# Seven products in place of eight for the second half of the first tokens' gates, with the plan of the weight conversions redrawn

## The chip, the core and the metric

The kernel runs on one core of one Trainium2 chip. TensorE (PE) multiplies, with its weight loads (PEld) beside the products; VectorE (DVE) and ScalarE (ACT) do everything elementwise; SyncE (SP) issues nearly all DMAs, in order. The metric is device time in microseconds (us), the median of several executions; one further execution was profiled.

## The reference, cut

```python
# attention: 4 batches, 12 heads, 448 tokens, head size 64, with 12x12 mixes of the heads
scores = mix(scale * q @ k.T, w_pre); attn = mix(softmax(scores), w_post); x = attn @ v   # 1792 x 768
# first feed-forward part, d_ff 1536
y = (sigmoid(x @ w_gate) * (x @ w_val)) @ w_out            # 1792 x 768
# second feed-forward part, d_ff 2048
h = y @ w_in;  out = (h * sigmoid(1.702 * h)) @ w2_out
```

The five feed-forward weights come as 64-bit numbers, and everything is computed in 32 bit.

## The kernel before

After the attention, class `Ffn` works on the tokens in two halves of 2 x 448: `first(0)`, `first(1)`, then `second(1)`, `second(0)`. All is laid out with features on the 128 partitions and 448 tokens in a row.

**Products.** Each 32-bit operand is split into a high part and a rest, and each product is three passes on PE (high by high, high by rest, rest by high). A *block* here is one weight tile `w`, 128 rows x 3 x 128 columns, high and rest. `product` (L871) is the plain form: it uses a block for 18 matmuls of 448 columns. `quarters` (L918) is a form of Strassen's kind: a 2 x 2 arrangement of blocks is done in seven products of sums instead of eight, each block used for 9 matmuls. Its operands are sums of weight blocks (`sum`) and sums of activations (the lists `A[p]`), and its outputs are put together from partial sums in PSUM: ACT copies some out (`save`, L923), DVE adds (`finish`, L927).

**Who uses which form.** In `first(0)` all 12 gate blocks f are plain: 48 weight blocks, tiles `pg` and `pv`. `first(1)` uses `quarters` for its six pairs of f, 84 blocks. `py` (w_out) is plain for both halves, 24 blocks each. `second` uses `quarters` for w_in (four groups of 14 blocks each time) and another form of seven products, `po`, for w2_out.

**Where a block comes from.** A weight piece is loaded as 64-bit words into `ws` (`stage`, five buffers), converted to 32 bit (ACT twice in `bits`; DVE three times in `conv1` to `conv3`), stored to DRAM as `kept`, and, if it is used at once, split by ACT (`high`) and DVE (`low`, L807) into `w` (five buffers). 136 pieces are converted in all. Pieces that are not used at once (`whole(.., False)`) are only stored, between those that are; for `first(0)` these are pieces of w2. Later uses load `kept` again. An order written out in `__init__` (`units`) fixes all of this, and `split`, called by `ahead` after each product, emits it some blocks ahead of PE. Each engine runs its list in order.

`sums_out` makes sums of w2_out's blocks in `first(1)` and `second(1)` and stores them; `next_a` and `next_y` make the lists `A` for the next stage.

## Time and profile before

| what | value |
|---|---|
| median of 3 runs | 1388.9 us (1388.85 to 1389.53) |
| the profiled execution, its own time | 1390.18 us |
| its span, first to last instruction | 1388.1 us |
| PE busy, of the span | 1367.1 us, 98% |
| DVE busy | 1049.7 us, 76% |
| ACT busy | 891.1 us, 64% |
| 16 DMA queues of q1, share of the span | 54.5% |
| bytes moved | 242.36 MB |
| TensorE clock granted | 0.999 |

The profiled execution is 1.3 us longer than the median. An engine's busy time counts an instruction from its start to the end of its writes, and the starts of neighbours overlap the ends, so the distance between two starts is what an instruction costs in a dense row.

### The profile page before, as it was taken

How to read it: one execution, taken by the hardware profiler on the slowest of the kernel's cores; microseconds unless marked ns; L12 is line 12 of the kernel's file. 1: busy time of each engine (PE TensorE's matmuls, PEld its weight loads, DVE VectorE, ACT ScalarE, POOL GpSimd, SP SyncE). 2: the span in 40 equal slices, each digit the busy share in tenths (PEclk: the TensorE clock that was granted, in tenths of full speed). 3: DMA queues.
4: the chain of work that ended last, by engine and by line, in shares of the span. 5: the costliest groups of instructions: out<-in, count | busy, mean ns of one | idle time of the engine just before them, and what ended most of it. 6: DMA issues, size and time to landing. Idle time of an engine off the chain costs nothing.

```text
span 1388.1 us, 26019 instructions
## 1 busy us (share of the span) xinstructions
PE 1367.1 (98%) x8976; PEld 1248.3 (90%) x8976; DVE 1049.7 (76%) x2425; ACT 891.1 (64%) x2087; POOL 168.2 (12%) x159
## 2 busy tenths in 40 slices
PE   7999999999999999999999999999999999999998
PEld 5888888888888999999999988999889999999998
DVE  5777677867888788887868888785877679567654
ACT  5877688878888677676755555563666355566352
POOL 2443344434430000000000000000000000000000
PEclk9999999999999999999999999999999999999999
DMA  6644534622536588887973542683652587222574
GB/s 155 193 139 131 153 126 132 198 98 73 167 116 209 176 292 270 277 294 253 301 245 101 175 140 70 212 281 114 197 167 69 164 268 255 65 69 74 158 252 154
DMA packets 213699, 242.36 MB, mean 175 GB/s; under 512 B 69420, under 2 KB 201280, under 8 KB 213568
## 3 DMA queue, kind: packets, MB, share of 16 engines
q1 hardware_dynamic: 212544, 240.47, 54.5%
q8 instruction: 70, 1.15, 0.3%
q14 instruction: 61, 0.50, 0.1%
q10 hardware_dynamic: 960, 0.23, 0.1%
q0 software_dynamic: 64, 0.01, 0.0%
HBM read 149.04 MB, written 53.08 MB: 146 GB/s over the span
## 4 chain that ended last, share of the span: by engine, by line
PE 84%; DVE 8%; ACT 3%; DMA 2%; issue 2%; POOL 0%; SPq 0%; DVEq 0%; ACTq 0%; POOLq 0%
PE pq L918 20%; PE po L1312 15%; PE py L871 13%; PE pso L328 8%; PE pg L871 6%; PE pv L871 6%; PE psp L283 5%; PE psv L347 5%; PE psq L243 5%; ACT ex L297 1%; DMA gt<-sc 1%; PE pst L208 1%; DVE st L290 1%; DVE w L807 1%; DMA xy<-kept 1%
## 5 line engine op out<-in xcount | busy, mean ns | idle before, releaser
L918 PE MATMUL pq<-xy,w 128*128 128x448 f32 x1764 | 361.8, 366 | 3.4 <-DVE w L807 3.4
L918 PEld LDWEIGHTS pq<-xy,w 128*128 128x128 f32 x1764 | 330.3, 188 | 34.4 <-DVE w L807 6.2
L1312 PE MATMUL po<-wf,xy 128*128 128x384 f32 x1200 | 209.3, 336 | 0.0
L1312 PEld LDWEIGHTS po<-wf,xy 128*128 128x128 f32 x1200 | 209.0, 188 | 0.1
L276 POOL TENSOR_TENSOR ghl<-gt,ghl 120x448 fp32r<-120x448 f32 (+1 forms) x143 | 163.5, 1148 | 240.6 <-ACT ghl L212 179.3
L328 PEld LDWEIGHTS pso<-w,ex 120*112 120x112 f32 (+1 forms) x1440 | 159.3, 177 | 23.2 <-ACT w L310 6.5
L871 PE MATMUL py<-xy,w 128*128 128x448 f32 x864 | 175.1, 364 | 0.0
L328 PE MATMUL pso<-w,ex 120*112 120x120 f32 (+1 forms) x1440 | 172.6, 270 | 2.5 <-ACT w L310 1.6
L871 PEld LDWEIGHTS py<-xy,w 128*128 128x128 f32 x864 | 162.0, 187 | 12.8
L283 PE MATMUL psp<-ghl,wphl 120*120 120x448 f32 x540 | 140.2, 385 | 1.4 <-DVE at L212 0.8
L290 DVE TENSOR_REDUCE st<-psp 120x1 f32<-120x448 f32 x180 | 109.0, 614 | 33.6 <-PE psp L283 32.9
L297 ACT ACTIVATE ex<-psp,st 120x448 f32<-120x448 f32 x180 | 113.2, 635 | 10.7 <-DVE st L290 3.6
L745 ACT ACTIVATE wc<-ws 128x384 f32<-128x384 f32 x136 | 75.5, 555 | 67.0 <-DMA ws<-in_moe_w_in_dram 26.2
L899 ACT CAST xy<-xy 128x384 fp32r<-128x384 f32 (+1 forms) x176 | 79.3, 472 | 42.9 <-DVE xy L1044 42.8
L283 PEld LDWEIGHTS psp<-ghl,wphl 120*120 120x120 f32 x540 | 89.3, 183 | 14.2 <-issue 2.0
L900 DVE TENSOR_TENSOR xy<-xy 128x384 fp32r<-128x384 f32 (+1 forms) x176 | 85.6, 504 | 14.3 <-ACT xy L899 13.9
L871 PE MATMUL pg<-xy,w 128*128 128x448 f32 x432 | 90.3, 366 | 0.0
L871 PE MATMUL pv<-xy,w 128*128 128x448 f32 x432 | 89.5, 365 | 0.0
L871 PEld LDWEIGHTS pv<-xy,w 128*128 128x128 f32 x432 | 81.2, 188 | 6.4
L871 PEld LDWEIGHTS pg<-xy,w 128*128 128x128 f32 x432 | 80.9, 188 | 6.5
L212 ACT CAST ghl<-gt 120x448 fp32r<-120x448 f32 (+1 forms) x131 | 73.7, 569 | 13.1 <-PE psp L283 9.8
L347 PEld LDWEIGHTS psv<-at,vt 112*64 112x64 f32 x1536 | 73.7, 137 | 5.4 <-issue 2.5
(91 smaller groups left out, 1940.2 us busy)
## 6 DMA issues: line engine op xcount, KB each, us to landing
gt<-sc SPq DMA_DIRECT2D x172, 210.0 KB
kept<-wc SPq DMA_DIRECT2D x136, 192.0 KB
ws<-kept SPq DMA_DIRECT2D x68, 384.0 KB
wf<-sb SPq DMA_DIRECT2D x64, 384.0 KB
ws<-in_moe_w_out_dram SPq DMA_DIRECT2D x56, 384.0 KB
ws<-in_moe_w_in_dram SPq DMA_DIRECT2D x32, 384.0 KB
sb<-xy SPq DMA_DIRECT2D x32, 384.0 KB
wf<-kept SPq DMA_DIRECT2D x64, 192.0 KB
```

The costliest lines, as they stand in the source:

```text
L276: eng.tensor_tensor(out=t[:m, 1], in0=gt.pop(s)[:m], in1=t[:m, 0].bitcast(F32), op=ALU.subtract)
L283: nc.tensor.matmul(ps[:m, :S], wphl[:m, wp, :m], t[:m, gp], start=(i == 0), stop=(i == 2))
L290: nc.vector.tensor_reduce(out=st[:m, 0:1], in_=pre[s][:m, :S], axis=AX.X, op=ALU.max, negate=True)
L297: nc.scalar.activation(t[:m], pre.pop(s)[:m, :S], AF.Exp, bias=st[:m, 0:1], scale=1.0, accum_out=st[:m, 1:2])
L328: nc.tensor.matmul(ps[:JC, c, :, :n], e[:m, c * JC:(c + 1) * JC], w[:m, :, :n], start=True, stop=True)
L347: nc.tensor.matmul(ps[a * 64:a * 64 + 64, r, :n], vt[b][:, g, c, :], a_t[:, c, g, :n], start=(c == 0), stop=(c == NJ - 1), tile_position=( ...
L745: self.nc.scalar.activation(c.bitcast(F32), st[:, :, 1].bitcast(F32), AF.Abs, scale=self.DOWN)
L871: self.nc.tensor.matmul(acc[hb][:, :self.S], st, act[k0 + kc][hb][:, ap], start=(k0 + kc == 0 and part == 0 and ap == 0), stop=(k0 + kc == ...
L899: self.nc.scalar.copy(dst[:, 0], src)
L900: self.after(n, lambda: self.nc.vector.tensor_tensor(out=dst[:, 1], in0=src, in1=dst[:, 0].bitcast(F32), op=ALU.subtract))
L918: nc.tensor.matmul(x, st, A[p][c][:, ap], start=(first and c + part + ap == 0), stop=(c == self.KG - 1 and part == 1), skip_group_check=no ...
L1312: nc.tensor.matmul(acc[:, :PW], x[:, part], w[:, wp], start=(start and part == 0 and wp == 0), stop=(stop and part == 1), skip_group_check ...
```

## The change

1. Only the first six f of `first(0)` stay plain (`DIRECT`). The other six go as three groups of `quarters`, with a list `A` for these tokens (`widen`). Their 24 weight pieces (`early`) are converted during the first six f and the first groups, stored, and loaded back as whole groups into four activation-sized blocks (`lift`); `own_sum` makes the weight sums in place there. The six groups of `first(1)` use the same way.
2. The conversions of w2 move later: three in the last group of `first(0)`, 13 beside its `py`, three in each group of `first(1)`, and 30 beside the second `py`.
3. The gate outputs of f = 0 and 1 (`SPILL`) are stored to DRAM (`gd`), loaded back before `py`, and split there; `py` uses them last.
4. In `quarters` the order of the seven products is 1, 5, 6, 2, 7, 3, 4. Product 1 is copied by ACT into the PSUM bank of output 2, and products 2 and 4 end in PSUM, where ACT or DVE reads them directly: two adds of DVE instead of four for each gate or value (in `second(0)` the first two groups keep an add for product 2).
5. `sums_out` of `first(1)` is spread over 38 places instead of 55 and ends by f = 5.

```diff
-    ORDER = (1, 2, 6, 5, 7, 4, 3)
+    SPILL = 2
+    DIRECT = 6
+    ORDER = (1, 5, 6, 2, 7, 3, 4)
...
+        def kept_own(j, others):
+            loads = [[4 * (j + f) + 2 * g for f in range(2)] for g in range(2)]
+            after = max(where[i + x] for y in loads for i in y for x in range(2)) + 2
+            self.groups.append((loads, after))
+            n = len(self.groups) - 1
+            spread = [len(others) * min(x, 8) // 8 for x in range(15)]
+            for x, (p, g) in enumerate((p, g) for p in self.ORDER for g in range(2)):
+                self.used.append(len(self.units))
+                self.units.append(("o", (n, g), p))
+                convert(*others[spread[x]:spread[x + 1]])
+
+        early = [*range(4 * D, o1)]
+        for i in range(4 * D):
+            where[i] = len(self.units)
             whole(i)
-            if 6 <= i < o1 and (i % 3 or i in (12, 36)) or i > o1 + 4 and i % 2:
-                whole(rest.pop(0), False)
+            if i >= 5 and i % 3:
+                convert(early.pop(0))
+        for n, j in enumerate(range(D, K1, 2)):
+            m = (6, 5, 0)[n]
+            convert_now = [early.pop(0) for _ in range(min(m, len(early)))]
+            if j == K1 - 2:
+                convert_now += [rest.pop(0) for _ in range(3)]
+            kept_own(j, convert_now)
...
+    def lift(self):
+        n = len(self.kblocks)
+        if n < min(self.allowed, len(self.groups)) and self.step > self.groups[n][1] and len(self.blocks) >= 4 + self.spare:
+            self.kblocks.append([[self.form(F32) for _ in range(2)] for _ in range(2)])
+            for mine, loads in zip(self.kblocks[n], self.groups[n][0]):
+                for x, i in zip(mine, loads):
+                    self.nc.sync.dma_start(x[:, :, :self.PW], self.kept[i // 2].rearrange("a p f -> p a f"))
...
+    def keep_gate(self, t, f, h, x):
+        if f < self.SPILL:
+            self.nc.sync.dma_start(self.gd[t][f][h], x)
+        else:
+            self.G[f][h] = self.form()
+            self.spare -= 1
+            self.hilo(self.G[f][h], x)
...
-                if bank == 1:
-                    save(q, p)
-                if p == 2:
+                if p == 1 and seeded:
+                    acc[q][2] = self.banks("pq", 1)[0]
+                    nc.scalar.copy(acc[q][2][:, :S], x)
+                elif p in (1, 5, 6):
+                    save(q, p, x)
+                elif p == 2 and seeded:
+                    done(q, 0, 0, x)
+                elif p == 2:
                     finish(q, 1, x, 0, 0)
                 elif p == 7:
-                    finish(q, 7, acc[q][5][:, :S], 1, 1, x)
-                elif p == 4:
-                    finish(q, 7, x, 0, 1)
+                    finish(q, 5, x, 1, 1)
                 elif p == 3:
                     finish(q, 6, x, 1, 0)
+                else:
+                    done(q, 0, 1, x)
...
+    def widen(self):
...
+        def sums(c):
+            (x1, x3), (x2, x4) = ((x[:, 0], x[:, 1]) for x in raw[c])
+            self.tt(x4, x3, x4, ALU.add)
+            self.tt(x3, x1, x3, ALU.subtract)
+            self.tt(x1, x4, x1, ALU.subtract)
+            self.tt(x2, x2, x1, ALU.subtract)
```

On PE the attention and all later stages keep their rows. The end of `first(0)` and what follows stood so before (`pg`, `pv` are gates and values, the `pq` of L918 are the groups of `first(1)`):

```order
L871 MATMUL pg<-xy,w 128x448 x36
L871 MATMUL pv<-xy,w 128x448 x36
L871 MATMUL py<-xy,w 128x448 x432
L918 MATMUL pq<-xy,w 128x448 x756
L871 MATMUL py<-xy,w 128x448 x432
```

and now, after six pairs of such `pg` and `pv` rows where there were twelve:

```order
L956 MATMUL pg<-xy,w 128x448 x36
L956 MATMUL pv<-xy,w 128x448 x36
L1011 MATMUL pq<-xy,w 128x448 x378
L956 MATMUL py<-xy,w 128x448 x432
L1011 MATMUL pq<-xy,w 128x448 x756
```

Twelve rows of 36 matmuls have become one of 378.

On DVE, in the first six f of `first(0)`, this stood from one gate's product with its value (`sg`) to the next block (`w`); `wc` are the conversions:

```order
L894 TENSOR_TENSOR sg<-sg,pv 128x448 x2
L758 SCALAR_TENSOR_TENSOR wc<-wc,ws 128x384
L753 TENSOR_SCALAR wc<-wc 128x384
L764 SCALAR_TENSOR_TENSOR wc<-ws,wc 128x384
L900 TENSOR_TENSOR xy<-sg,xy 128x448 x2
L758 SCALAR_TENSOR_TENSOR wc<-wc,ws 128x384
L753 TENSOR_SCALAR wc<-wc 128x384
L764 SCALAR_TENSOR_TENSOR wc<-ws,wc 128x384
L807 TENSOR_TENSOR w<-wc,w 128x384
```

and now this (the `xy<-xy` rows are `widen`: four sums, and the rests of its splits):

```order
L993 TENSOR_TENSOR xy<-xy 128x448 x2
L979 TENSOR_TENSOR sg<-sg,pv 128x448 x2
L795 SCALAR_TENSOR_TENSOR wc<-wc,ws 128x384
L790 TENSOR_SCALAR wc<-wc 128x384
L801 SCALAR_TENSOR_TENSOR wc<-ws,wc 128x384
L993 TENSOR_TENSOR xy<-xy 128x448 x2
L993 TENSOR_TENSOR xy<-sg,xy 128x448 x2
L795 SCALAR_TENSOR_TENSOR wc<-wc,ws 128x384
L790 TENSOR_SCALAR wc<-wc 128x384
L801 SCALAR_TENSOR_TENSOR wc<-ws,wc 128x384
L878 TENSOR_TENSOR w<-wc,w 128x384
L1141 TENSOR_TENSOR xy<-xy 128x448 x4
```

The conversions are as dense as before, and `widen`'s rows stand between them.

On SP, in the same stretch, stores of converted pieces and loads of the next ones alternated:

```order
L767 DMA kept_116<-wc 128x384
L735 DMA ws<-in_moe_w_out_dram 128x768
L767 DMA kept_69<-wc 128x384
L735 DMA ws<-in_moe_w_gate_dram 128x3x256
L767 DMA kept_117<-wc 128x384
```

Now the loads of a whole group come between, soon after the store that fills the last of its pieces (and, elsewhere in the stretch, 12 loads `xy<-xd` for `widen`):

```order
L804 DMA kept_76<-wc 128x384
L772 DMA ws<-in_moe_w_gate_dram 128x3x256
L804 DMA kept_69<-wc 128x384
L772 DMA ws<-in_moe_w_gate_dram 128x3x256
L852 DMA xy<-kept_73 128x2x384
L852 DMA xy<-kept_75 128x2x384
L852 DMA xy<-kept_74 128x2x384
L852 DMA xy<-kept_76 128x2x384
L804 DMA kept_77<-wc 128x384
```

The loads of `kept_73` to `kept_76` stand ahead of the next pieces' loads, and the last of them reads what was stored four rows above the first.

## Rows read from the trace of the kernel before

**Rows 1.** The page: span, and busy time of each engine

```profile
span 1388.1 us, 26019 instructions
PE 1367.1 (98%) x8976; PEld 1248.3 (90%) x8976; DVE 1049.7 (76%) x2425; ACT 891.1 (64%) x2087; POOL 168.2 (12%) x159
```

**Rows 2.** The chain that ended last: start, length, engine, tile, line, instructions

```profile
468.12 7.30 PE pv L871 x36
...
635.93 87.40 PE py L871 x432
...
1177.61 102.42 PE pq L918 x504
```

**Rows 3.** Waits of PEld, 723 to 880 us: total, times, longest

```profile
PEld pq L918 <- DVE w L807: 2.5, 4, 1.1
```

**Rows 4.** Timeline of PEld, 723 to 1075 us: idle before a piece in brackets

```profile
805.28 25.59 PEld L918 LDWEIGHTS pq<-xy,w 128*128 128x128 f32 x126 [0.68 <-DVE w L807]
...
833.83 45.43 PEld L918 LDWEIGHTS pq<-xy,w 128*128 128x128 f32 x223 [1.08 <-DVE w L807]
...
989.47 1.71 PEld L918 LDWEIGHTS pq<-xy,w 128*128 128x128 f32 x9 [2.22 <-DVE w L807]
```

**Rows 5.** Waits of PEld, 967 to 1073 us

```profile
PEld pq L918 <- DVE w L807: 3.7, 4, 2.2
```

**Rows 6.** Timeline of DVE, 521.8 to 526.9 us: start, length

```profile
521.38 0.62 DVE L894 TENSOR_TENSOR sg<-sg,pv 128x448 f32<-128x448 f32 x1
521.91 0.55 DVE L758 SCALAR_TENSOR_TENSOR wc<-wc,ws 128x384 uint32<-128x384 uint32 x1
522.38 0.36 DVE L753 TENSOR_SCALAR wc<-wc 128x384 f32<-128x384 f32 x1
522.65 0.55 DVE L764 SCALAR_TENSOR_TENSOR wc<-ws,wc 128x384 uint32<-128x384 uint32 x1
523.12 0.55 DVE L807 TENSOR_TENSOR w<-wc,w 128x384 fp32r<-128x384 f32 x1
523.58 0.56 DVE L758 SCALAR_TENSOR_TENSOR wc<-wc,ws 128x384 uint32<-128x384 uint32 x1
```

**Rows 7.** `low` (L807) on DVE: stretch, length, busy (count), clock, DMA share, GB/s

```profile
0.00:504.60 504.60, 7.75 (x14) 1.00 0.49 153
...
0.00:577.50 577.50, 19.40 (x35) 1.00 0.54 169
```

**Rows 8.** Matmuls of `product` (L871) on PE by the same times

```profile
0.00:504.60 504.60, 44.75 (x217) 1.00 0.49 153
...
0.00:577.50 577.50, 117.65 (x577) 1.00 0.54 169
```

**Rows 9.** Busy time by stretch: PE, PEld, DVE, ACT, POOL; then clock, DMA share, GB/s

```profile
519.00:548.00 29.00, 29.00 (x144) 26.88 (x144) 24.65 (x56) 19.65 (x43) 0.00 (x0) 1.00 0.81 270
...
679.00:708.00 29.00, 29.00 (x146) 26.87 (x145) 24.84 (x55) 19.92 (x44) 0.00 (x0) 1.00 0.96 314
705.00:710.00 5.00, 5.00 (x26) 4.64 (x25) 1.88 (x5) 2.52 (x6) 0.00 (x0) 1.00 1.06 392
...
775.50:801.50 26.00, 25.79 (x127) 23.40 (x126) 24.15 (x49) 15.71 (x34) 0.00 (x0) 1.00 0.56 173
...
937.00:967.04 30.04, 30.04 (x150) 27.85 (x149) 14.31 (x27) 8.93 (x19) 0.00 (x0) 1.00 0.38 131
```

**Rows 10.** The page's DMA issues: count, KB each

```profile
kept<-wc SPq DMA_DIRECT2D x136, 192.0 KB
...
ws<-in_moe_w_gate_dram SPq DMA_DIRECT2D x24, 384.0 KB
...
xy<-xd SPq DMA_DIRECT2D x24, 224.0 KB
```

**Rows 11.** Timeline of DVE, 966 to 1020 us, one wait for a DMA

```profile
986.17 1.15 DVE L1044 TENSOR_TENSOR xy<-xy 128x384 f32<-128x384 f32 x2 [2.88 <-DMA xy<-kept]
```

**Rows 12.** The chain, two loads that stood in it

```profile
979.89 6.19 DMA xy<-kept
1004.43 4.66 DMA xy<-kept
```

More of the change, by code (lines that the diff above doesn't have):

```diff
@@ L563, in __init__ @@
         for m in range(KD):
-            self.pieces += [self.block(w_out, k0, KG, m * 128, 128) for k0 in range(0, K1, KG)]
+            self.pieces += [self.block(w_out, k0 % K1, KG, m * 128, 128) for k0 in range(KG, K1 + KG, KG)]
         for f in range(K2):
@@ L1131, in first @@
     def first(self, t):
[L1133 to L1134 removed]
+        K1, S, D = self.K1, self.S, self.DIRECT
+        G = self.G = [[None, None] for _ in range(K1)]
         if t:
[L1136 to L1141 removed]
+            self.later_work(self.sums_out(range(3), 3), 38)
+        else:
+            self.A = {p: [] for p in self.ORDER}
+            self.later_work(self.widen(), 4 * D - 7)
+            self.spare = 12
+        for f in range(K1):
+            if t or f >= D:
+                if f % 2:
+                    self.spare = 0 if f < self.SPILL else 4
+                    if f < K1 - 1:
+                        self.allowed += 1
+                    self.gates(t, f - 1, f == K1 - 1)
+                if t and f == 5:
                     self.rush()
[L1143 removed]
+            else:
                 if f == 0:
```

195 lines of the change are left out of this document (138 added, 57 removed).

## The prediction

> **What bounds the kernel.** The page comes first: PE is busy for 1367.1 of 1388.1 us and PEld for 1248.3, while DVE has 76% and ACT 64% [rows 1]. Then the chain of waits, where from 468 us on hardly anything but PE stands: 36 matmuls of a gate or a value take 7.30 us, which is 0.2027 us each, the 432 of `py` 87.40, and 504 of `quarters` without a wait 102.42, which is 0.2032 each [rows 2]. A matmul more or less is therefore worth 0.203 us as long as nothing else stops PE. Third, what does stop it: in `first(1)` PEld waited four times for the rests of weight blocks (`low`, L807), 2.5 us in all [rows 3], in pieces of 0.68 and 1.08 us where one group of seven products passes to the next [rows 4]; in the first groups of `second(1)` four times again, 3.7 us [rows 5], of which 2.22 in one piece [rows 4] that followed a 2.88 us wait of DVE for a load of `sums_out` [rows 11]. In all of these stretches DVE is late, not PE slow.
>
> So DVE's list needs a measure. Its rows overlap at their ends, so I take the distance of starts: 0.47 us for each of the two long steps of a conversion, 0.27 for the short one, 0.46 for a `low`, 0.53 for 448 columns [rows 6]; other operations on 384 columns I take as 0.47. One conversion is 1.21 us. With these I count, block by block in the order of DVE's list, what it must do while PE uses a block (18 matmuls, 3.65 us, in plain products; 9, 1.82 us, in `quarters`).
>
> **What the change takes away.** 12 rows of 36 matmuls go, 432 x 0.2027 = 87.6 us; 378 come, 378 x 0.2032 = 76.8 us. That is -10.8 us, and no other stage gains or loses a matmul.
>
> **What it puts on DVE in `first(0)`.** In the first six f the list was comfortable: in the 13 blocks from the 15th on there stood 22 conversions, 13 `low` and 16 operations of 448 columns, 41.1 us, for 47.4 us of PE. Now the same 13 blocks hold 18 conversions, 15 of 384 columns and 36 of 448 (`widen`'s sums and splits and the sums of the first pair's gates), 47.6 us. The last four of them are blocks of 9 matmuls, so PE needs 9 x 3.65 + 4 x 1.82 = 40.1 us. DVE is 7.5 us over. What it has in hand: at 504.6 us 14 `low` had started where PE had used 217 / 18 = 12.1 blocks, at 577.5 us 35 against 577 / 18 = 32.1 [rows 7, 8], so 2 to 3 blocks, 7.3 to 11 us. A DVE that never waited would just pass. It does wait: in the densest stretch of `first(1)` it was busy for 24.15 of 26.0 us, 93%, and PE waited there [rows 9]. At 95%, 47.6 us become 50, 10 over, and 0 to 2.7 us of PE time are lost; to that come the small waits of a full list. The two groups behind hold 44.4 us for 51; their densest four blocks, 9.1 and 7.5 us for 7.3 of PE, are like the group ends of `first(1)` (9.0 for 7.3), which cost 0.7 to 1.1 us each. I take 3 us for the passage and 1 for the two groups: +4. Bounds: 0, if the hand of 3 blocks holds; 10, if it counts for nothing.
>
> **What it puts on the DMA queues.** In the 20 blocks of f = 1 to 5 SP issues 33 pieces of 384 KB and 33 stores of 192 KB as before, and besides 12 loads and 4 stores of 224 KB and one group of four times 384 KB [rows 10]: 24.7 MB in 73.0 us, 338 GB/s. The busiest long stretch moved 314 GB/s at a share of 0.96 [rows 9], so a full share is some 327, and 24.7 MB take 75.5 us, 2.5 over. That comes out of the same 2 to 3 blocks in hand; a late piece makes ACT wait, then DVE. It is in the +4. The Trainium skill (DMA: Bandwidth & Descriptors, Specifications) gives some 358 GB/s from memory for one core; by that the stretch would take 69.0 us, an estimate, and no load would be late. The trace does not hold to it in the short: 5 us went at 392 GB/s [rows 9]. By that limit the rival without new waits, below, gains.
>
> Beside the first `py` DVE's list grows from 66.8 to 73.5 us of 87.6, and the DMAs to 30.2 MB (35 conversions, 28 transfers of 224 KB, two groups), 92.3 us at 327 GB/s against 87.4 [rows 2]. Five over, seven in hand: I take +0.5, bounds 0 and 5.
>
> **What the new order does to `first(1)` and `second(1)`.** Two adds of four go and two conversions a group come; the sums are 130.6 us before and 131.3 now, of 153. But the heap at the end of a group (nine operations of 448 and nine of 384 columns in four blocks, 9.0 us for 7.3) is taken apart: 6.5 us now. In the first three groups `sums_out`, squeezed into fewer places, gives 8.7 us at worst. I take -0.5 us of the 2.5 lost there, bounds -2 and +3. In `second(1)` the first two groups hold 49.9 us instead of 48.8. More to the point, at the end of the second `py` DVE was idle half the time, 14.31 us busy of 30.04 [rows 9], and now has the last conversions of w2 there: the last four blocks of `py` and the first four behind them hold 24.4 us of work instead of 16.3, for 21.9 of PE. What is queued behind are the splits by `next_y` that product 5, now second, needs 4.9 us after `py` ends. +0.5 us, bounds -1 and +4.
>
> **At nothing**: ACT's copy into PSUM (the third bank is read one pair later, 3.65 us, and a copy was there before); the gates by way of DRAM, used after 9 of 12 steps of `py`, 11 us after it begins; the loads of later groups, issued 7 to 14 blocks, 13 to 25 us, before use, where such a load took 4.7 to 6.2 us [rows 12]. Without that cover each would cost PE what the load in rows 11 did, some 2 us.
>
> **Sum.** -10.8 + 4 + 0.5 - 0.5 + 0.5 = -6.3 us. The profiled execution took 1390.2 us, so 1383.9; it stands 1.3 us above the median, so 1382.6 for the median. Less than 0.2%, 2.8 us, can't be told from no change here.
>
> **The rivals.**
>
> *No new wait.* The three blocks in hand carry DVE over the passage, and the flatter group ends free 1.5 us more: 1388.9 - 10.8 - 1.5 = 1376.6. For it: PE never waited between 468 and 723 us. Against: DVE never had more work than PE there. 17%.
>
> *DVE becomes the bound of `first(0)`.* The hand counts for nothing, since SP, which issues in order, waits for DVE's conversions and the group's stores before the next piece's load; 10 us lost there, 1388. For it: both lists and queues are over at the same blocks. Against: behind the passage the load falls to 44.4 of 51 us. 13%, a little under half of it faster by more than 2.8 us.
>
> *Slower: groups are loaded too late.* ACT runs in order; if its `high` for a group's first block waits for `lift`'s loads, the copies out of PSUM behind it wait too, and PE stops at the product that reuses the bank. The places are the second and third group of `first(0)` and the first of `first(1)`, whose loads follow the conversions they read, in a full queue. At the 6.19 us of the longest load in the chain [rows 12], three cost 18.6 us, 1401; at 4 us each 1394.6. It decides from 2.1 us each on (no gain) and makes the kernel slower by 0.2% from 3 us. For it: store, landing and four loads of 384 KB must pass in 13 us. Against: the first two loads are all that the first blocks need. 12%.
>
> **The numbers.** My forecast has 58%, from 1379 to 1386. The low end of the range is that of the first rival, 1376; the high end, 1389, takes in the second and leaves out the third, 12%, and little else. Faster by over 0.2%: 58 + 17 + 6 = 81%. Within: 7 of the second, 2 of the third, 9%. Slower: 10%.
>
> **What would show it.** One row of 378 matmuls in some 77 us, with `first(0)` from 468 us to the start of `py` in about 161 (168 before). Waits of PE or PEld for `low` between the 15th and the 28th block, near 515 to 560 us, 2 to 4 us together, and few later; none for ACT's copies. DMA share near 1 in f = 1 to 5. Waits in `first(1)` near 2 us, and in the first three groups alone. I am wrong if the wait stands elsewhere (at `xy<-kept`, or at the start of `second(1)` by more than 4 us), if there is none, or if matmuls themselves take longer beside fuller queues.

## The result and the profile after

The changed kernel takes 1407.7 us (1402.9 to 1407.8) against 1388.9 (1388.3 to 1389.5): ratio 1.0127, 95% interval 1.0105 to 1.0149. It is slower by 1.3%, where 0.5% faster was forecast. The profiled execution is the shortest of them, 1402.9 us; what makes the other three 4.8 us longer is open, since they left no trace (their mean granted clocks are 0.990, 0.990 and 0.992, this one's 0.993).

The page of the changed kernel: span, engines, and the row of `py`, with what PE waited for at its end.

```profile
span 1400.9 us, 26068 instructions
...
PE 1362.5 (97%) x8922; PEld 1240.3 (89%) x8922; DVE 1067.2 (76%) x2451; ACT 909.5 (65%) x2135; POOL 168.5 (12%) x159
...
L956 PE MATMUL py<-xy,w 128*128 128x448 f32 x864 | 183.3, 373 | 11.8 <-DVE xy L942 5.9
```

PE is busy for 4.6 us less than in [rows 1], not for 10.8. What stands behind that shows in the stages; a cut at the first weight load of each gives these windows (the columns are those of [rows 9]).

```profile
467.20:634.40 167.20, 160.60 (x776) 146.03 (x775) 145.02 (x307) 109.91 (x235) 0.00 (x0) 0.99 0.70 228
634.40:730.30 95.90, 91.43 (x433) 82.66 (x432) 79.34 (x174) 61.27 (x132) 0.00 (x0) 0.96 0.92 306
730.30:884.40 154.10, 154.10 (x757) 141.82 (x757) 135.13 (x276) 100.83 (x215) 0.00 (x0) 1.00 0.52 174
884.40:983.30 98.90, 91.54 (x433) 82.79 (x433) 73.96 (x157) 52.03 (x112) 0.00 (x0) 0.95 0.81 269
983.30:1085.80 102.50, 102.50 (x506) 94.56 (x505) 76.50 (x158) 67.51 (x150) 0.00 (x0) 1.00 0.44 144
```

From top to bottom: the first tokens' gates, the first `py`, the second tokens' gates, the second `py`, the first product with w2. The stages that were to stay as they were moved most (forecast by the prediction's terms):

| Stage, us | before | after | difference | forecast |
|---|---|---|---|---|
| first tokens' gates, from the first `pv` | 167.8 | 167.2 | -0.6 | -6.8 |
| first `py` | 87.4 | 96.0 | +8.6 | +0.5 |
| second tokens' gates | 156.3 | 154.1 | -2.2 | -0.5 |
| second `py` | 87.4 | 98.9 | +11.5 | 0 |
| first w2 product | 106.0 | 102.5 | -3.5 | +0.5 |
| before and behind these | | | -0.9 | 0 |

The sum is +12.8 up to rounding, the difference of the spans, 1400.9 and 1388.1. The medians lie 18.8 us apart; the 6 us more are the place of the two profiled executions among the others, and the table does not account for them. The two `py` lose 20.0 us. PEld's timeline shows where in the first:

```profile
634.37 10.92 PEld L956 LDWEIGHTS py<-xy,w 128*128 128x128 f32 x54
646.68 0.19 PEld L956 LDWEIGHTS py<-xy,w 128*128 128x128 f32 x1 [1.39 <-ACT xy L944]
647.40 0.19 PEld L956 LDWEIGHTS py<-xy,w 128*128 128x128 f32 x1 [0.53 <-ACT xy L944]
649.82 0.19 PEld L956 LDWEIGHTS py<-xy,w 128*128 128x128 f32 x1 [2.23 <-DVE xy L942]
650.35 1.60 PEld L956 LDWEIGHTS py<-xy,w 128*128 128x128 f32 x5 [0.35 <-DVE xy L942]
653.77 0.29 PEld L956 LDWEIGHTS py<-xy,w 128*128 128x128 f32 x1 [1.81 <-DVE xy L942]
654.30 7.69 PEld L956 LDWEIGHTS py<-xy,w 128*128 128x128 f32 x32 [0.25 <-DVE xy L942]
```

54 matmuls run, nine of the twelve steps of k (10.9 us). The tenth needs gate 0, and PE waits six times, 6.6 us, first for its cast (L944, ScalarE), then for its low part (L942, VectorE). ScalarE in turn waited for the load, and SP issued that load late. SP's, then ScalarE's timeline:

```profile
639.92 0.32 SPq L804 DMA_DIRECT2D kept<-wc  x1
...
640.81 2.54 SPq L1301 DMA_DIRECT2D xy<-gd  x4
```

```profile
646.06 0.56 ACT L944 CAST xy<-xy 128x448 fp32r<-128x448 f32 x1 [4.50 <-DMA xy<-gd]
```

The four loads stand at 640.81, 6.4 us after `py` began, behind stores of converted weights that each wait for VectorE. SP's own waits, 634 to 645 us (total, times, longest):

```profile
SPq L804 <- DVE wc L801: 4.8, 4, 1.9
```

The second `py` repeats it, later still, after waits of 1.9 us for a gate made last (L992, L993; experiment 2); PEld, then SP:

```profile
894.67 0.30 PEld L956 LDWEIGHTS py<-xy,w 128*128 128x128 f32 x2 [1.54 <-ACT xy L992]
895.33 1.71 PEld L956 LDWEIGHTS py<-xy,w 128*128 128x128 f32 x9 [0.36 <-DVE xy L993]
900.86 0.29 PEld L956 LDWEIGHTS py<-xy,w 128*128 128x128 f32 x1 [3.82 <-ACT xy L944]
901.44 0.28 PEld L956 LDWEIGHTS py<-xy,w 128*128 128x128 f32 x1 [0.30 <-ACT xy L944]
904.93 0.29 PEld L956 LDWEIGHTS py<-xy,w 128*128 128x128 f32 x1 [3.20 <-DVE xy L942]
```

```profile
894.18 2.59 SPq L1301 DMA_DIRECT2D xy<-gd  x4
```

The waits are 6.6 and 9.5 us, the losses 8.6 and 11.5. The other 2 us each go with matmuls at a lower clock. Windows of 5 us, first `py`:

```profile
640.00:645.00 5.00, 5.00 (x26) 4.62 (x26) 3.74 (x8) 1.01 (x2) 0.00 (x0) 1.00 0.94 297
645.00:650.00 5.00, 1.79 (x7) 0.83 (x5) 2.16 (x5) 3.79 (x9) 0.00 (x0) 1.00 1.05 380
650.00:655.00 5.00, 3.74 (x9) 2.42 (x10) 5.00 (x13) 3.79 (x8) 0.00 (x0) 0.54 0.83 273
655.00:660.00 5.00, 5.00 (x22) 4.53 (x21) 3.59 (x9) 2.96 (x7) 0.00 (x0) 0.78 0.95 306
660.00:665.00 5.00, 5.00 (x26) 4.65 (x25) 4.93 (x11) 3.61 (x9) 0.00 (x0) 1.00 0.82 261
```

While PE stood for 3.2 of 5 us the granted clock was 1.00; in the next 5 us it was 0.54, which is near the lower level of 1.2 GHz, then 0.78, then 1.00, the upper level of 2.4 GHz, again. In the second `py` it was 0.50 and 0.52 from 900 to 910 us, behind the longest waits. In the kernel before nothing stopped PE in either `py`, and the granted clock of both is 1.00.

In the first tokens' gates the waits stand where they were forecast, from 517 to 563 us, but they are 8.9 us and not 2 to 4, and two of the six are for ScalarE's part of a block (L872) and not for `low` (L878):

```profile
517.21 2.73 PEld L956 LDWEIGHTS pv<-xy,w 128*128 128x128 f32 x14 [1.83 <-DVE w L878]
...
529.64 6.38 PEld L956 LDWEIGHTS pv<-xy,w 128*128 128x128 f32 x32 [1.59 <-DVE w L878]
537.21 3.54 PEld L956 LDWEIGHTS pg<-xy,w 128*128 128x128 f32 x18 [1.20 <-ACT w L872]
543.19 0.70 PEld L956 LDWEIGHTS pg<-xy,w 128*128 128x128 f32 x4 [2.45 <-ACT w L872]
544.27 4.29 PEld L956 LDWEIGHTS pg<-xy,w 128*128 128x128 f32 x14 [0.38 <-DVE w L878]
...
563.36 2.72 PEld L1011 LDWEIGHTS pq<-xy,w 128*128 128x128 f32 x14 [1.41 <-DVE w L878]
```

### The profile page after: what moved, and what is told of

It is laid out like the page before. It is cut to its first block, busy times and chain, and to the rows that moved or that the text cites. A ratio compares the mean times of both kernels' runs of the same rounds, so it can differ in the third digit from the quotient of the medians.

```text
span 1400.9 us, 26068 instructions
## 1 busy us (share of the span) xinstructions
PE 1362.5 (97%) x8922; PEld 1240.3 (89%) x8922; DVE 1067.2 (76%) x2451; ACT 909.5 (65%) x2135; POOL 168.5 (12%) x159
## 4 chain that ended last, share of the span: by engine, by line
PE 57%; DMA 1%; DVE 1%; issue 0%; ACT 0%; SPq 0%; DVEq 0%; ACTq 0%
PE pq L1011 30%; PE po L1468 15%; PE py L956 12%; DMA xy<-gd 1%; DMA ws<-in_moe_w_in_dram 0%; DVE wc L801 0%; DVE wc L795 0%; ACT wc L782 0%; DMA ws<-in_moe_w_val_dram 0%; DVE xy L942 0%; DVE wc L790 0%; DVE w L878 0%; SPq L772 0%; SPq L804 0%; ACT xy L944 0%
## 5 line engine op out<-in xcount | busy, mean ns | idle before, releaser
L1011 PE MATMUL pq<-xy,w 128*128 128x448 f32 x2142 | 436.8, 365 | 1.0 <-DVE w L878 1.0
L1011 PEld LDWEIGHTS pq<-xy,w 128*128 128x128 f32 x2142 | 401.7, 188 | 35.5 <-DVE w L878 1.4
L956 PE MATMUL py<-xy,w 128*128 128x448 f32 x864 | 183.3, 373 | 11.8 <-DVE xy L942 5.9
L956 PEld LDWEIGHTS py<-xy,w 128*128 128x128 f32 x864 | 165.5, 192 | 29.4 <-DVE xy L942 8.1
L992 ACT CAST xy<-xy 128x384 fp32r<-128x384 f32 (+2 forms) x188 | 85.5, 479 | 41.0 <-DVE xy L1141 39.5
L993 DVE TENSOR_TENSOR xy<-xy 128x384 fp32r<-128x384 f32 (+2 forms) x188 | 92.6, 512 | 19.0 <-ACT xy L992 18.8
L1141 DVE TENSOR_TENSOR xy<-xy 128x384 f32<-128x384 f32 (+1 forms) x144 | 79.5, 559 | 6.6 <-DMA xy<-kept 4.8
L347 PE MATMUL psv<-at,vt 112*64 112x120 f32 (+1 forms) x1536 | 77.1, 260 | 0.6 <-ACT ex L297 0.4
L878 DVE TENSOR_TENSOR w<-wt,w 128x384 fp32r<-128x384 f32 x100 | 54.8, 553 | 28.8 <-ACT w L872 28.8
L790 DVE TENSOR_SCALAR wc<-wc 128x384 f32<-128x384 f32 x136 | 48.3, 355 | 37.2 <-ACT wc L782 36.8
```

What stands on the lines that cost most here:

```text
L347: nc.tensor.matmul(ps[a * 64:a * 64 + 64, r, :n], vt[b][:, g, c, :], a_t[:, c, g, :n], start=(c == 0), stop=(c == NJ - 1), tile_position=( ...
L956: self.nc.tensor.matmul(acc[hb][:, :self.S], st, act[k0 + kc][hb][:, ap], start=(k0 + kc == 0 and part == 0 and ap == 0), stop=(k0 + kc == ...
L992: self.nc.scalar.copy(dst[:, 0], src)
L993: self.after(n, lambda: self.nc.vector.tensor_tensor(out=dst[:, 1], in0=src, in1=dst[:, 0].bitcast(F32), op=ALU.subtract))
L1011: nc.tensor.matmul(x, st, A[p][c][:, ap], start=(first and c + part + ap == 0), stop=(c == self.KG - 1 and part == 1), skip_group_check=no ...
L1141: self.nc.vector.tensor_tensor(out=dst, in0=x, in1=y, op=op)
```

## The experiments

Stage times below are cut as in the table above, in its order, so a wait for the first weight of a stage counts to the stage ahead of it. Each is from one execution. What stands ahead of the first `pv` has the same rows in every kernel, and yet `pv` begins anywhere from 465.0 to 471.1 us in the profiled executions, a range of the size by which whole times of one kernel differ (2 to 9 us); the stages leave this out. Each compared kernel keeps all of the change but what its edit says, unless it is put on the kernel before. "Ratio" is to the kernel before, executed beside it (its medians were 1389.8 to 1390.6 us there), with its 95% interval; it is not the quotient of the two medians.

**1. The reload issued sooner (`gates_back_sooner`).** The loads move from behind the last group of gates into it:

```diff
+                    if last is not True and p == last:      # p == 5
+                        self.bring()                        # the four loads of gd
...
-        for f in range(self.SPILL):
-            for h in range(2):
-                G[f][h] = self.form()
-                self.nc.sync.dma_start(G[f][h][:, 1].bitcast(F32), self.gd[t][f][h])
```

> The changed kernel, with one thing moved: the four loads that bring the two spilled gates back are issued inside the last group of gates, after its second product, instead of behind that group's last stores of converted weights. Theory A (the reload is late: it is issued 6.2 and 9.6 us after the first py step begins, ScalarE's cast of it stands ahead of the weights' casts, and TensorE's clock falls while it waits): both py stages go back from 96.0 and 99.2 us to 87.5 to 90 each, no wait of TensorE's loads there is over 0.5 us, and the whole is 15 to 20 us below the changed kernel's 1407.7, so 1388 to 1393. Rival B (the py stages are longer since more conversions lie beside them, 35 and 29 in place of 33 and 19, and the reload only happens to be late): both stages stay above 94 us and the whole at 1400 to 1408.

Measured: 1396.2 us, ratio 1.0046 (1.0030 to 1.0062); stages 168.0, 93.4, 154.2, 93.6, 102.7. The two `py` got back 8 of their 20 us and lie between what the two theories gave. In the first `py` the loads are now in time, and yet the low parts are not. ScalarE, VectorE and PEld:

```profile
646.14 1.03 ACT L944 CAST xy<-xy 128x448 fp32r<-128x448 f32 x2
```

```profile
650.15 1.16 DVE L942 TENSOR_TENSOR xy<-xy 128x448 fp32r<-128x448 f32 x2
...
654.11 1.16 DVE L942 TENSOR_TENSOR xy<-xy 128x448 fp32r<-128x448 f32 x2
```

```profile
654.78 0.29 PEld L956 LDWEIGHTS py<-xy,w 128*128 128x128 f32 x1 [2.51 <-DVE xy L942]
```

ScalarE casts at 646.1 without a wait for the load. VectorE, in the order of its list, comes to the low parts at 650.2 and 654.1, where PE wants gates 0 and 1 from 650.4 on: conversions stand ahead of them, and it was busy for 10.4 of the 11.0 us since `py` began.

**2. No reload (`no_reload`).** Loads, casts and low parts are left out; gates 10 and 11 stand in:

```diff
+        used = G[self.KG:] + [G[10], G[11], G[2]]
...
-            for k, _ in enumerate(self.product(py, act)):
+            for k, _ in enumerate(self.product(py, used)):
```

> The changed kernel without the reload: the gates of blocks 0 and 1 are still stored to DRAM but not brought back, not cast, and gates 10 and 11 are used a second time in their place (this leaves those two gates out of the product with w_out). Everything else stands as in the changed kernel, the conversions beside py too. Theory A: both py stages 87.4 to 88.5 us, the whole 17 to 20 us below the changed kernel, 1387.5 to 1391; what it is faster than the kernel with the loads issued sooner is what the reload costs even when it is in time (I expect under 2 us). Rival B: the stages stay above 94 us, the whole above 1400.

Measured: 1388.9 us, ratio 0.9991 (0.9978 to 1.0004); stages 167.0, 87.4, 155.5, 89.5, 102.7. Both `py`:

```profile
632.20:719.60 87.40, 87.40 (x433) 81.03 (x432) 73.93 (x163) 56.65 (x123) 0.00 (x0) 1.00 0.96 318
875.10:964.60 89.50, 88.05 (x434) 80.95 (x434) 70.42 (x151) 49.38 (x108) 0.00 (x0) 1.00 0.88 287
```

All conversions stand beside `py` as in the changed kernel (73.9 us of VectorE's work in the first), and PE is never without work in the first. So theory A holds and rival B falls: the return of two gates' outputs costs 8.5 and 9.4 us. The expectation that a return in time costs under 2 us falls as well: with the loads sooner the kernel is 7.3 us above this one. The 2.1 us left in the second are a wait for the cast of gate 10, made last and now used eighth.

**3. Casts and low parts sooner too (`gates_split_sooner`).**

```diff
+                    if last == "gates" and p == 7:
+                        self.settle()          # cast and low part of the four blocks
...
-                if m == 0 and k in (self.KG - 1, 2 * self.KG - 1):
-                    for h in range(2):
-                        x = G[k // self.KG][h]
-                        self.part(self.nc.scalar, x, 0)
-                        self.after(0, lambda x=x: self.part(self.nc.vector, x, 1))
```

> The changed kernel with the reload issued inside the last group of gates, as in the run with the loads sooner, and with the reloaded gates' four casts on ScalarE and four low parts on VectorE also put inside that group, behind its fifth product, in place of behind the third and the sixth step of py. Theory A2 (with the loads in time, the waits that stay in py, 3.3 and 5.0 us, are for low parts that stand in VectorE's list behind conversions; VectorE has no idle time from 634 to 660 us, and a low part ends at 651 and 655 us where it is wanted at 650 and 652): both py stages go from 93.4 and 93.6 to 87.5 to 89.5 us, the whole to 1388 to 1391. Rival B (VectorE has too much to do there, wherever the low parts stand): the wait moves to the weights' low parts, and the stages stay at 92 us or more, the whole at 1394 to 1398.

Measured: 1395.2 us, ratio 1.0029 (1.0009 to 1.0049); stages 167.9, 89.1, 156.9, 91.9, 103.2. The two `py` gain 6 us more, as expected of the first, not quite of the second; there one wait of 3.22 us for the cast of gate 10 stays. But the stage behind the first `py` is 2.7 us longer, with three waits, 2.9 us in all, at its start, two of them for VectorE, and the whole time is that of rival B, not clearly below experiment 1, whose interval overlaps: what `py` gained is in part lost behind it.

**4. The new order and the two outputs in PSUM alone (`quarters_only`)**, put on the kernel before:

```diff
-    ORDER = (1, 2, 6, 5, 7, 4, 3)
+    ORDER = (1, 5, 6, 2, 7, 3, 4)
...
+                if p == 1 and seeded:
+                    acc[q][2] = self.banks("pq", 1)[0]
+                    nc.scalar.copy(acc[q][2][:, :S], x)
...
-    EASE = {1: 1.1, 2: 0.4, 6: 2.0, 5: 2.0, 7: 0.5, 4: 0.4, 3: 0.6}
+    EASE = {1: 1.0, 5: 1.0, 6: 2.0, 2: 0.8, 7: 0.8, 3: 0.4, 4: 1.0}
```

`EASE` sets how much of the work in waiting (here `sums_out`) is issued behind each product. It comes with the order, and so does an earlier place of two loads of each group; the changed kernel has both.

> The kernel before, with the new order of the seven products and the two outputs that are summed in PSUM, and nothing else of the change: all first tokens' gates direct, no gate by way of DRAM, the conversions where they were. Theory A: the 2.6 and 3.6 us by which the changed kernel's seven-product stages (gates of the second tokens, first w2 product) are shorter come from this edit, so about 1382 to 1384, ratio 0.995 to 0.9965, and both stages show no wait of TensorE over 0.5 us. Rival B: they come from the kept weights' blocks and the fewer conversions that the other edits leave there; then this is 1388 to 1390, ratio 0.999 to 1.001, and the waits of the kernel before (four of 0.5 to 0.8 us in a group) are still there.

Measured: 1388.0 us, ratio 0.9974 (0.9959 to 0.9989); stages 167.8, 87.4, 156.3, 87.4, 102.8. The w2 product has the whole 3.2 us, in one piece without a wait:

```profile
968.90:1071.70 102.80, 102.80 (x506) 94.67 (x506) 76.37 (x158) 67.75 (x150) 0.00 (x0) 1.00 0.44 143
```

The second tokens' gates have nothing of it: four waits, 2.5 us in all, are there as before, but only two of them still for `low` (now L810). The other two are for ScalarE's sigmoid of a gate (L968). PEld, 725 to 882 us:

```profile
PEld pq L921 <- DVE w L810: 1.5, 2, 0.7
PEld pq L921 <- ACT s L968: 1.0, 2, 0.7
```

Half of each theory: nearly all of the 3.5 us comes from this edit, and the 2.2 us of the gates need the others as well.

**5. The first tokens' gates: four cuts, and two of them together (`light_no_x`).** Each leaves the reload as it is, so the stage tells, not the whole.

```diff
 no_x_loads: sums of the quarters from the high parts in SBUF
-                    self.nc.sync.dma_start(x[:, h], self.xd[h][:, cc, :])
 sums_gpsimd: the sums of widen on another engine
+            tt = lambda dst, x, y, op: self.nc.gpsimd.tensor_tensor(out=dst, in0=x, in1=y, op=op)
 half_early: six of thirteen conversions ahead left out
+                if x // 2 not in (13, 15, 17):
+                    convert(x)
 early_light: conv1 and conv2 left out for all thirteen
+        if self.units[i][0] == "f" and not 24 <= self.units[i][2] < 37:
```

`no_x_loads`:

> The changed kernel, where the sums of the tokens' quarters for the seven products are formed from the rounded high parts that are in SBUF, in place of twelve loads of the whole values from DRAM (this leaves the low parts out of these sums). VectorE's and ScalarE's instructions stay as many and as large; 2.75 MB of transfers between about 490 and 545 us are gone. Theory A (the six waits of 8.9 us in sum there, and the half clock behind them, come from full DMA queues: the share is 0.92 to 0.96 with 304 to 325 GB/s from 468 to 540 us): the stage up to py goes from 167.4 to 157 to 161 us, the whole to 1397 to 1401. Rival B (VectorE's list, 0.96 of the stretch, and the sums of 2.6 us that stand ahead of a conversion): the stage stays at 165 us or more and the whole within 3 us of the changed kernel.

`sums_gpsimd`:

> The changed kernel, with the twelve sums of the tokens' quarters (VectorE, 2.60 us for four) on GpSimd, which does nothing else there; the reload is as in the changed kernel. Theory A (VectorE's list sets the waits of the direct products between 511 and 563 us): 7.8 us of VectorE's work are gone, the waits fall from 8.9 us to under 5 and the stage up to py from 167.4 to 160 to 164, the whole to 1400 to 1404. Rival B (what is late there are the weights' loads: ScalarE waits 3.2 us for one at 533 us, and the transfers were not relieved enough by leaving out the tokens' loads): the stage stays at 166 us or more and the whole within 2 us of 1407.7.

`half_early`:

> The changed kernel, six blocks direct, with six of the thirteen pieces that are converted ahead beside the direct products left out (this puts the values of six other pieces of the gate weights in their place in the seven-product groups). The tokens' sums, loads and parts stay. Theory A (the conversions ahead fill VectorE's list): 6 x 1.4 us = 8.4 us of VectorE's work less in 73 us of products; the waits between 511 and 563 us fall from 8.9 us to under 3 and the stage up to py from 167.2 to 158 to 161 us. Rival B (the tokens' sums and parts, or the loads, make them): the waits stay at 6 us or more and the stage at 164 us or more.

`early_light`:

> The changed kernel with two of VectorE's three conversion instructions left out (0.27 and 0.47 us each) for the thirteen pieces that are converted ahead beside the direct products, so that the weights kept of these have wrong values. Their loads, ScalarE's two instructions, the third of VectorE and the stores stay. Theory A (VectorE's list sets the waits): 9.6 us less of VectorE's work, the transfers as they were; the waits between 511 and 563 us fall from 8.9 us to under 4, and the stage up to py from 167.2 to 158 to 162 us. Rival B (the transfers and the staging buffers of the pieces do it, and leaving out six pieces helped since 3.5 MB went with them): the stage stays at 164 us or more.

`light_no_x`:

> The two earlier cuts together, with six blocks direct and the reload as in the changed kernel: the tokens' twelve loads for the sums left out (the low parts with them), and two of VectorE's three conversion instructions left out for the thirteen pieces converted ahead (their kept values are wrong). Alone, the first took the stage up to py from 167.2 to 166.2 us, the second to 165.2. Theory C (two causes in a row: VectorE's list holds the pieces up to 535 us, and the transfers, with the conversion behind them, hold those from 535 us on; with one of them gone the other still makes ScalarE and the loads late): together 157.5 to 161.5 us, far more than the 164.2 that the two sums give. Rival D (the two add up, and something else, ScalarE's waits for the conversions' chain through the staging buffers, keeps the rest): 163 to 165 us, waits of 6 us or more still there.

Measured, stage up to `py` and waits of 0.3 us or more in it: the changed kernel 167.2 and 8.9; `no_x_loads` 166.2 and 8.1; `sums_gpsimd` 167.4 and 7.3 with the first wait at 500 us; `half_early` 158.0 and 0.9; `early_light` 165.2 and 8.3; `light_no_x` 164.9 and 6.6. Whole times: 1403.2, 1402.6, 1392.2, 1406.1 and 1400.9 us, the last three from one execution each, the first two with ratios of 1.0089 (1.0064 to 1.0114) and 1.0095 (1.0080 to 1.0110).

Only `half_early` does what theory A said, and it has the whole gain: 9.8 of 10.8 us, with one wait of 0.88. So the number of conversions ahead sets the waits. The others have the stages of their second theory (B, or D); the whole times of `no_x_loads` and `sums_gpsimd` are 4.5 and 5.1 us below the changed kernel's median, more than B allowed, and beside its profiled execution, 1402.9, the same. What of a conversion does it is told in part by the others. With less work on VectorE the first two waits shrink from 1.83 and 1.59 to 0.49 and 0.62 (`early_light`), and with the tokens' loads gone too they vanish; those up to 535 us are VectorE's list, helped by the full queue. The later ones stay in both. `light_no_x`, SP, ScalarE and PEld:

```profile
519.36 2.14 SPq L852 DMA_DIRECT2D xy<-kept  x4
...
522.38 0.38 SPq L772 DMA_DIRECT2D ws<-in_moe_w_val_dram  x1
```

```profile
529.60 0.55 ACT L782 ACTIVATE wc<-ws 128x384 f32<-128x384 f32 x1 [3.85 <-DMA ws<-in_moe_w_val_dram]
```

```profile
533.85 3.54 PEld L956 LDWEIGHTS pg<-xy,w 128*128 128x128 f32 x18 [1.32 <-ACT w L872]
539.59 0.71 PEld L956 LDWEIGHTS pg<-xy,w 128*128 128x128 f32 x4 [2.19 <-ACT w L872]
```

SP issues the first group's four loads of 384 KB at 519.4; ScalarE then waits 3.85 us for a piece of w_val, until 529.6, and PE stands until 533.85, and again until 539.59. The changed kernel has ScalarE's wait with 3.21 us, `half_early` with 3.89. There PE does not wait: when ScalarE's wait began, VectorE had finished 1.8 blocks more than PE had used (`low` rows against weight loads / 18), where the changed kernel had 0.7.

The second of these waits of PE has one more cause, the sums that the rival of `no_x_loads` names. VectorE, then ScalarE, in `light_no_x`:

```profile
535.38 2.35 DVE L1141 TENSOR_TENSOR xy<-xy 128x448 f32<-128x448 f32 x4
...
538.38 0.55 DVE L801 SCALAR_TENSOR_TENSOR wc<-ws,wc 128x384 uint32<-128x384 uint32 x1
```

```profile
539.03 0.51 ACT L872 CAST w<-wc 128x384 fp32r<-128x384 f32 x1 [2.59 <-DVE wc L801]
```

VectorE, held up by the late piece, has four sums of the tokens in its list ahead of the next conversion, and ScalarE's cast, for which PE stands until 539.59, waits for that conversion. The same rows of the changed kernel are 2.60 and 2.84 us. In `sums_gpsimd`, where these sums are not on VectorE, PE has no wait of 0.3 us from 531.7 to 558 us.

So theory C falls, and the numbers are those of D, 6 us or more of waits. Its cause is not shown alone: what is left goes with `half_early`, which leaves out six pieces whole (their loads, ScalarE's steps, VectorE's third step, the stores), and which of these does it was not separated. That the four loads alone make ScalarE's wait was not tried either, and stays open.

`sums_gpsimd` did not shorten the stage, since VectorE had no less to do. GpSimd, then VectorE:

```profile
499.84 5.60 POOL L1196 TENSOR_TENSOR xy<-xy 128x448 f32<-128x448 f32 x4 [1.56 <-DMA xy<-xd]
```

```profile
500.29 1.30 DVE L790 TENSOR_SCALAR wc<-wc 128x384 f32<-128x384 f32 x1
501.51 1.52 DVE L801 SCALAR_TENSOR_TENSOR wc<-ws,wc 128x384 uint32<-128x384 uint32 x1
...
505.58 0.55 DVE L801 SCALAR_TENSOR_TENSOR wc<-ws,wc 128x384 uint32<-128x384 uint32 x1
```

While GpSimd works, from 499.8 to 505.4, VectorE's conversion steps of 0.35 and 0.55 us take 1.30 and 1.50. (GpSimd's three groups of four sums took 5.3, 5.6 and 12.1 us.) VectorE is busy for 143.0 us from 468 to 630 where the changed kernel has 140.2.

**6. Eight or ten blocks direct, and the gates' return mended.** The groups of seven products cost a head start of conversions; fewer groups, fewer conversions.

```diff
-    DIRECT = 6
+    DIRECT = 8                                   # or 10
-            if i >= 5 and i % 3:
+            if i >= 5 and i % 2:                 # with 10: i % 4 == 0
 d8_last: gates made last are used last
-        act = G[self.KG:] + G[:self.KG]
+        act = G[3:9] + G[:3] + G[9:]
 d8_last_b: loads behind product 1, casts and low parts behind 2 (fourth), not 5 and 7
```

> The changed kernel with eight blocks of the first tokens' gates direct and four as two groups of seven products, in place of six and three groups: 396 products of a bank in place of 378, so 3.65 us more of TensorE's work, but only 16 pieces to convert ahead in place of 24, and 32 pieces' time for them. The reload is as in the changed kernel. Theory A (the conversions ahead overfill VectorE's list in the direct stretch): its waits fall from 8.9 us to under 3, the stage up to py from 167.4 to 163 to 166 us, the whole to 1402 to 1406. Rival B (the waits come with the sums and parts of the tokens, whenever these are made): the waits stay at 7 us or more and the stage goes to 169 to 171 us, the whole to 1409 to 1412.

> The two together: eight blocks direct, and the reload with its casts and low parts inside the last group of gates. If the two causes are apart from each other the gains add: py 87.5 to 89.5 us each, the stage up to py 163 to 166, the whole 1383 to 1388, ratio 0.996 to 0.999 to the kernel before. If one is only hidden by the other, it stays above 1390.

> Eight blocks direct, the reload with casts and low parts inside the last group of gates, and in py the pieces of w_out in the order gates 3 to 8, 0 to 2, 9 to 11, in place of 3 to 11, 0 to 2, so that the gates that are made last are used last. Theory A3 (what stays in the second py, 91.8 us with one wait of 2.84 us for ScalarE's cast of gate 10, is that the change put the last-made gates at the eighth of twelve steps): the second py goes to 87.5 to 89 us, the whole from 1388.5 to 1384.5 to 1386.5. Rival B (ScalarE's list is late there by itself): a wait of the same size at another tile, and the whole at 1387 to 1390.

> The same with the reload issued behind the first product of the last group, and its casts and low parts behind the fourth, in place of the second and the fifth. If the 1.28 us that TensorE waits at the start of the first py (for a low part of a weight, behind the four low parts of gates) comes from those four standing late in the group, it goes, and the whole is 1 to 2 us below the kernel with the later place; if VectorE's list is full there wherever they stand, the wait moves into the last group and the time is the same within 1 us.

> Ten blocks direct, and one group of seven products for the first tokens: 414 products of a bank, only 8 pieces converted ahead; else as the kernel with eight. Theory A (with eight blocks two waits of some 1.5 us in the first tokens' gates are left to gain, and each group less costs 3.65 us): the stage up to py is 164 to 165 us against 162.4 with eight, the whole 1.5 to 3 us above the kernel with eight. Rival B (the conversions beside the direct products still cost more than the waits show, in py behind them too): the whole is the same or lower.

| Kernel | us | ratio, interval | stages |
|---|---|---|---|
| `direct_8` | 1399.6 | 1.0068, 1.0053 to 1.0084 | 163.0, 95.2, 153.5, 96.9, 103.3 |
| `split_and_direct_8` | 1388.5 | 0.9995, 0.9984 to 1.0006 | 162.4, 88.7, 157.8, 91.8, 103.7 |
| `d8_last` | 1389.2 | 0.9995, 0.9983 to 1.0008 | 163.6, 88.8, 157.2, 90.1, 106.5 |
| `d8_last_b` | 1386.1 | 0.9974, 0.9961 to 0.9986 | 163.5, 87.6, 155.0, 88.7, 105.0 |
| `d10_last` | 1388.0 | 0.9979, 0.9964 to 0.9994 | 164.2, 88.7, 155.1, 89.2, 104.6 |

`direct_8` has the stage and the waits of theory A (3.65 us more of products, 4.2 us less of stage, 2.3 us of waits); its whole time is below the 1402 to 1406 expected. The two causes nearly add: `split_and_direct_8` lies 19 us below the changed kernel, where the gains one by one are 12.5 and 8.1, and just above the range expected. With the order of w_out's pieces (`d8_last`) the wait for gate 10 is gone, and the second `py` itself takes what A3 expected. The 90.1 of the table holds a wait for the first weight of the product behind it. PEld:

```profile
879.75 87.51 PEld L956 LDWEIGHTS py<-xy,w 128*128 128x128 f32 x432
...
969.84 0.34 PEld L1011 LDWEIGHTS pq<-xy,w 128*128 128x128 f32 x2 [2.58 <-ACT w L872]
```

That is rival B, a wait of the same size (2.84 before) at another tile, and the whole is B's too; the stage behind is 2.8 us longer. The earlier place of casts and low parts (`d8_last_b`) has a median 3.1 us lower, with intervals that just touch: this wait is 1.16 there and the stage behind 105.0. The 1.28 us at the start of the first `py` went into the last group of gates, as 0.99, which is the second reading of its expectation; the time is not. `d10_last`, which has the loads and casts where `d8_last` has them, is 1.2 us below that with overlapping intervals, so rival B holds: no gain from eight over ten is shown. Four blocks by seven products save 7.3 us of products; `d8_last_b` is 1.9 us shorter in these five stages than `quarters_only`, and their ratios are equal.

**7. The tokens' parts in the new order.** The change reordered the products and left the order in which the quarters' parts are made.

```diff
 next_y, beside the second py (quarter_a, beside the first, likewise)
-            self.hilo(A[2][c], x)
             self.tt(t1, t1, y, ALU.add)
+            self.hilo(A[5][c], t1)
             self.tt(t0, t1, t0, ALU.subtract)
-            self.flush()
             self.hilo(A[6][c], t0)
+            self.hilo(A[2][c], x)
```

> Eight blocks direct, gates back behind the first and split behind the fourth product, last-made gates last; and the tokens' quarters are split into high and low parts in the order in which the new sequence of products uses them (1, 5, 6, 2, 7, 3, 4), where the changed kernel kept the order of the sequence before. Theory A4 (the waits at the start of the second tokens' gates, 0.32 and 1.30 us, and of the first w2 product, 1.16, 1.49, 1.10 and 0.48 us, are for parts that stand in the old order): these fall under 2 us in sum, the whole from 1386.1 to 1382 to 1384.5. Rival B (VectorE and ScalarE have that list to work off there whatever stands first): the whole at 1385 to 1388.

> Eight blocks direct, gates back and split early, last-made gates last, and the order of the parts changed only where the second tokens' quarters are loaded and split beside the first py (there the new order took 0.6 us of the stage behind it), not where the outputs of the second py are split (there it made one wait of 4.79 us for ScalarE's cast of a weight). Expected: the first w2 product back to 105 us or less and the whole at 1384 to 1386.5, ratio 0.996 to 0.998. Rival: no difference to the kernel with the old order in both, 1386 to 1388, the spread between executions being larger than 0.6 us.

> The kernel before with the new order of the seven products and the outputs summed in PSUM alone, as in the run with this edit alone (ratio 0.9974), and the parts of the tokens' quarters in the order of their use. There the starts of the two stages showed no wait of 0.3 us or more, so I expect no more than 0.5 us from it: ratio 0.996 to 0.999. If the order of the parts matters by itself, it is 1 us or more below the run without it.

Measured: `d8_in_order` 1387.9 us, 0.9984 (0.9971 to 0.9996), stages 164.3, 87.6, 154.4, 92.6, 104.5; `d8_quarters_a` 1387.3, 0.9984 (0.9971 to 0.9997), stages 162.1, 87.6, 155.9, 88.4, 105.2; `quarters_in_order` 1385.9, 0.9971 (0.9957 to 0.9985), stages as `quarters_only`. Theory A4 falls: in `d8_in_order` the waits did not shrink, one of 4.79 us for a weight's cast came in their place, and all three intervals overlap those of the kernels with the old order. The stages of `quarters_in_order` and `quarters_only` are equal; the 5.1 us between their profiled executions all stand ahead of the first `pv`. The same order with ten blocks (`d10_in_order`), expected at 1384 to 1386.5, took 1389.3 (0.9991, 0.9980 to 1.0001). No version is shown to beat the two that are 0.3% below the kernel before, the edit of the order alone and `d8_last_b`.

## Why the prediction was wrong

**The step that failed** is the one under "At nothing": the gates by way of DRAM, "used after 9 of 12 steps of `py`, 11 us after it begins". The 11 us are right (10.9). But they were held against a transfer, and what had to fit in was SP's list up to the loads (6.4 us; 9.8 in the second `py`), the transfers (ScalarE had the first 5.3 us behind the issue), a cast in ScalarE's list and a low part in VectorE's. The price named for lost cover, some 2 us, was too small as well: 8.5 and 9.4 us (experiment 2). These are 17.9 of the 19.1 us between the forecast, -6.3, and +12.8 (by the spans; by the medians it is 25.1). The rest nearly cancels: 6.2 us more in the first tokens' gates and 2.1 for gate 10, against 7.1 us less than forecast elsewhere.

**"first(0), +4", bounds 0 and 10.** The place was right and the kind in part: 5.2 us of the waits are for `low`, 3.7 for ScalarE's casts behind a late piece and behind VectorE's sums. The size was at the upper bound: 10.2 us, since 10.8 of products went and 0.6 of the stage. 8.9 are waits; the clock, 0.70 from 545 to 550 us, makes most of the rest. I let VectorE's excess and the queue's 2.5 us come out of the same blocks in hand; but one wait of ScalarE for a piece behind the group's loads was 3.2 us by itself, and the hand was gone before it: PE waited for `low` at 517 us already. The rival "DVE becomes the bound" had the size, 10 us. The products' term itself, -10.8, is borne out by `half_early`: -9.8 with one wait of 0.88, in one execution.

**"first py, +0.5".** Right, once the return is out: 87.4 without it, in spite of 35 conversions and 318 GB/s.

**"first(1), -0.5" and "second(1), +0.5".** -2.2 and -3.5. The new order took the waits away wholly in the w2 product (experiment 4), where I expected the splits for product 5 to be late. In the second tokens' gates it left as much waiting as before; that flatter heaps at the ends of groups free the 2.2 us there, as I had read from [rows 4], is not shown.

**The second `py`** had no term. Its 11.5 us are 9.4 of the return and 2.1 of gate 10, made last and used eighth, which the new order of `act` brought.

**The rivals.** The slower one had the mechanism (ScalarE in order behind a load that is issued late, all that follows held) and came nearest in size, 1394.6 to 1401 against 1407.7, but it had the wrong load, which makes its size luck: for what `lift` loads ScalarE waited twice, 2.0 and 1.1 us, just ahead of the second tokens' gates, and PE not at all. It had 12%; the return of the gates, which is one more load with the same mechanism and a shorter cover, had none.

**The clock** was in no term. At 0.54 and 0.78 for 5 us each in the first `py`, and 0.50 and 0.52 in the second, it goes with the 2 us that each lost beyond its waits.

**The page's figure.** The Trainium skill (DMA: Bandwidth & Descriptors, Specifications) gives some 358 GB/s; by it no load would be late. The trace does not agree: from 500 to 520 us the queues moved 325 GB/s at a share of 0.96, and from 523.4 to 533.1 us, when ScalarE waited 3.2 us for a load, 319 GB/s at 0.97.

## What to carry to other kernels

An output that goes out to memory and comes back has a place in four lists that work in order: the queue that issues it, the transfers, the engine that casts it, the engine that splits it. Ask for each what stands ahead of it there; the time until its use is cover only as far as those lists are empty. And a saving in products is worth having only as far as the weights' conversions, which it moves closer together, keep their head start. With the return mended alike, six blocks by seven products stayed 0.3% above the kernel before (`gates_split_sooner`, 10.8 us less of products), and four came level with it (`split_and_direct_8`, 7.3 us less).

## What the runs showed of the hardware

VectorE and GpSimd hold each other up. With GpSimd adding two tiles in SBUF (5.60 us for four, 1.4 each; 12.1 us for another four), VectorE's steps became 0.95 us longer, those with one input too: 0.35 to 1.30, 0.55 to 1.50. The Trainium skill (Advanced Engine Details and Errata, GPSIMD Details) says that the two share a read and a write interface, in conflict where VectorE has two inputs in SBUF or works in a two-port mode; the trace agrees for the steps with two inputs, and in which mode the one-input step runs no run here shows. Moving 7.8 us of sums to an idle engine gave VectorE some 10.6 us of delay: 140.2 - 7.8 + 10.6 = 143.0.

The granted clock fell behind the first waits of `py` (1.00 while PE stood for 3.2 of 5 us, 0.54 in the next 5 us, in which it was busy for 3.7, then 0.78) and was at 1.00 again 10 us later. So 6.6 us of waits cost 8.6.
